# A second weight group's loads moved behind three activation loads, and its conversion behind the last unit's scaling, in a gated linear attention and feed-forward kernel

## The chip, the cores and the metric

One Trainium2 chip, one core. The metric is the device time of one launch in microseconds (us), lower is better. A reading is the median of several runs; the profile is one more execution, taken by the hardware profiler.

## The reference

Gated linear attention over 4 batches, 8 heads, 768 steps, 48 channels, then a feed-forward block with a leaky ReLU:

```python
for t in range(S):
    state = alpha[:, :, t, :, None] * state + np.einsum('bhd,bhe->bhde', k[:, :, t], v[:, :, t])
    y[:, :, t] = np.einsum('bhd,bhde->bhe', q[:, :, t], state)
...
x = np.ascontiguousarray(attn_out.transpose(0, 2, 1, 3)).reshape(B * S, H * D)   # 3072 x 384
h = x @ w_in                                                                    # w_in 384 x 2048
g = np.maximum(0.01 * h, h)
return (g @ w_out).astype(np.float32)                                           # w_out 2048 x 384
```

The weights arrive as 64-bit floats, all else as 32-bit ones.

## The kernel before

The steps are cut into 6 blocks of 128, and a **unit** is one block of one batch: 24 units, in the order block by block, batch by batch. Three units make one block of 384 rows for the feed-forward part, which takes the hidden width in 16 **weight groups** f of 128. One pair (block of rows i, weight group f) is an item: `ffn_in` (9 matmuls, L714), the leaky ReLU and the split of its result into a high and a low part (L719 to L728), `ffn_out` (9 matmuls, L743). A high part and two low ones give each product in three matmuls.

The attention of the first nine units, 0 to 8, runs ahead of nearly all feed-forward work; this stretch, some 65 us, is the one that the change touches. For one unit u:

- SyncE issues the loads: alpha, q and k (`load`, L151) and v (`load_values`, L170), 192 KB each. They go into ring buffers, so a load is issued when its buffer is free; "spare" is the third buffer of such a ring.
- TensorE transposes alpha, q and k (L303). VectorE scans alpha forward (`pc`, four short scans) and backward (`rc`, one long scan, in `scans`), and multiplies: `qs` = q times `pc` (`scaled_q`), `ks` = k times `rc` (`scaled_k`). A helper issues all of these, so they all stand as L288.
- TensorE makes the scores from `qs` and `ks` (L540); ScalarE copies them to `sm` (L420) and GpSimd zeroes their upper triangle (L422, both in `mask_scores`); TensorE transposes `ks` (`k_tokens`, L437), and ScalarE copies that and takes two sums (L441, L367).
- TensorE adds up the part of the past state (`past`), of the masked scores (`values`) and the new products (`products`), all L540; ScalarE and VectorE split the result into `large` (`split`, L554 and L288). After units 2, 5 and 8 two transfers inside the chip (`gather`, L603) bring the block of rows into place.

TensorE takes them in this order: scores(u), k_tokens(u), the transposes of u+1, past(u), values(u), products(u), scores(u+1).

Each weight group is loaded by five transfers on the same SyncE queue (`load_weights`): one of 384 KB of w_out (L228) and four of w_in (L224, 384 KB in all), into `raw`. Then it is **converted** from 64-bit to two 32-bit parts (`converting`, L241 to L280): ScalarE scales `raw` (L260) and takes the `signs` (L262); VectorE joins the `bits` (L266); ScalarE rounds them to the high part (L269); four VectorE operations (L273 to L280) give the low part.

A scheduler puts the instructions of every engine in an order, and the hardware keeps to it: each engine's queue is served in order. The kernel's text steers that order with `behind(key)`, which lets what stands in its block come behind a named earlier instruction of the same engine, and by the place at which the text gives an instruction out. Three tables do this for the first weight groups:

```python
LOADS = [(("v", 4), 0, 0), (("v", 5), 0, 1), (("v", 6), 1, None), (("g", 1), 2, None), (("v", 8), 3, None)]
AFTER = {0: ("sm", 5), 1: ("xh", 6), 2: ("sm", 8)}
BEGIN = ("sm", 5), ("xh", 6), ("kt", 8)
```

`LOADS` says behind which load a weight group's loads are issued: group 0 in two parts behind v of units 4 and 5, group 1 behind v of unit 6. `AFTER` puts the first ScalarE step of a conversion (L260) behind another ScalarE copy: for group 1 behind the split of unit 6. `BEGIN` says which instruction must have been given out before a conversion is.

Of the kernel before, what the change touches and what calls it, by code (L numbers as in the profile page):

```python
# [17 lines left out]
ALU = mybir.AluOpType  # L18
# [6 lines left out]
def gated_linear_attn_ffn(ctx, tc, q, k, v, alpha, w_in, w_out, out):  # L25
    nc = tc.nc
# [34 lines left out]
    AHEAD = 3 * UPB  # L61
# [54 lines left out]
    made = {}  # L116
# [3 lines left out]
    def behind(*key):  # L120

        return tc.issue_after(made[key].ins) if key in made else nullcontext()
# [7 lines left out]
    def load_next(u, i):  # L130

        for n in range(u + 1, u + 4):
            if n < NU and n - len(places(n, i)) == u:
                load(n, i)
# [28 lines left out]
    def load_values(u):  # L163
        if u >= NU:
            return
        if u >= AHEAD and later is not None:
            later.append((load_values, u))
            return
        tb, b = units[u]
        made["v", u] = nc.sync.dma_start(  # L170
            vals_sb[u % NV].rearrange("t (h d) -> t h d", h=H),
            v[b, :, tb * C:(tb + 1) * C, :].rearrange("h t d -> t h d"),
        )
# [58 lines left out]
    def put(ordered, eng, op, *args):  # L232

        if not ordered:
            return op(*args)
        line = lines[eng]
        with tc.issue_after(line[-1].ins) if line else nullcontext():
            line.append(op(*args))
        return line[-1]

    def converting(f, ordered=False):  # L241

        if f >= NF:
            return
        raw = jobs.pop(f)
        w_sb[f] = cst.tile([P, 2, 2 * DM], F32R, name=f"w{f}")
        hi, lo = w_sb[f][:, HIGH, :], w_sb[f][:, LOW, :]
        if not f64:
            val = raw[:, :, 0:P].bitcast(F32)
            hi, lo = (t.rearrange("p (g f) -> p g f", f=P) for t in (hi, lo))  # L250
            nc.scalar.copy(hi, val)
            made["w", f] = nc.vector.tensor_tensor(lo, val, hi.bitcast(F32), ALU.subtract)
            return
        words = raw.rearrange("p g (f w) -> p (g f) w", w=2)
        top, low = words[:, :, 1], words[:, :, 0]
        bits = cvp.tile([P, 2 * DM], I32, name="bits", bufs=NBITS)
        val = bits.bitcast(F32)

        with nullcontext() if lines["ACT"] else behind(*AFTER.get(f, ("hi", f - 1))):
            put(ordered, "ACT", lambda: nc.scalar.mul(top.bitcast(F32), top.bitcast(F32), 2.0 ** -112))  # L260
        yield
        put(ordered, "ACT", lambda: nc.scalar.copy(  # L262
            signs.bitcast(F16).rearrange("p (n w) -> p n w", w=2)[:, :, 1], top.bitcast(F32)))
        yield
        with nullcontext() if ordered else behind("w", f - 1):
            put(ordered, "DVE", lambda: nc.vector.scalar_tensor_tensor(  # L266
                bits, top, 3, signs, ALU.logical_shift_left, ALU.bitwise_or))
        yield
        made["hi", f] = put(ordered, "ACT", lambda: nc.scalar.copy(hi, val))  # L269
        yield  # L270
        pw = cvp.tile([P, 2 * DM], I32, name="pw", bufs=NPW)
        rest = pw.bitcast(F32)
        put(ordered, "DVE", lambda: nc.vector.tensor_scalar(pw, bits, -0x800000, None, ALU.bitwise_and))  # L273
        yield
        put(ordered, "DVE", lambda: nc.vector.tensor_tensor(val, val, hi.bitcast(F32), ALU.subtract))
        yield
        put(ordered, "DVE", lambda: nc.vector.scalar_tensor_tensor(
            rest, low.bitcast(U32), 2.0 ** -52, rest, ALU.mult, ALU.mult))
        yield
        made["w", f] = put(ordered, "DVE", lambda: nc.vector.tensor_tensor(lo, rest, val, ALU.add))  # L280

    def convert(f):
        for _ in converting(f):
            pass

    def vector(u, op, *args):

        return put(u >= AHEAD, "DVE", lambda: op(*args))  # L288
# [4 lines left out]
    def transposed(u, i, name, **kw):  # L293

        src = loaded(u, i)
        if u < AHEAD:
            ps = banks4()
            tiles = [ps[:, p, :] for p in range(NP)]
            if u == 0 and i == 0:
                other = ps_h.tile([P, 512], F32, name="ph").rearrange("r (p n) -> r p n", p=NP)  # L300
                tiles[NP // 2:] = [other[:, p, :] for p in range(NP // 2)]
            for p in range(NP):
                last = nc.tensor.transpose(  # L303
                    tiles[p], by_token(src)[:, 2 * p:2 * p + 2, :].rearrange("t h d -> t (h d)"), ident
                )
                if u == 0 and p % 2:
                    with tc.issue_after(last.ins):
                        keep_warm(WARM[2 * i + p // 2])
            return [ps, other] if u == 0 and i == 0 else ps
        t = atp.tile([P, NP, C], F32, name=name, **kw)  # L310
        src = src.rearrange("r (p n) -> r p n", p=NP)[:, :, 0:RUN]
        vector(
            u, nc.vector.transpose, t.rearrange("r p (j t) -> r p t j", t=T4),
            src.rearrange("r p (t d) -> r p t d", t=T4)[:, :, :, 0:32],
        )
        return t
# [11 lines left out]
    def every(t, first):  # L328
        return t.rearrange("r p (m s) -> r p m s", s=STEP)[:, :, :, first]

    def scans(u):
        aT = transposed(u, 0, "e", bufs=1)
        yield TURN
        pc, rc = (
            atp.tile([P, NP, C], F32, name=name, bufs=2 if u < AHEAD else 1) for name in (("pc", "rc") if u < AHEAD else ("up", "down"))
        )
        pe = ends_sb[u % 3]
        parts = aT if isinstance(aT, list) else [aT]
        n = NP // len(parts)
        for p in range(NP):  # L340
            vector(
                u, nc.vector.tensor_tensor_scan, pc[:, p, :], parts[p // n][:, p % n, :], ones.broadcast_to([P, C]), 1.0,
                ALU.mult, ALU.mult,
            )
        yield SCAN
        for part in parts:
            vector(u, nc.vector.memset, every(part[:, 0:n], 0), 0.0)
        vector(u, nc.vector.reciprocal, every(seed, STEP - 1), every(pc, STEP - 1))
        for at, part in zip(range(0, NP, n), parts):
            flat = [t.rearrange("r p t -> r (p t)") for t in (part[:, 0:n], seed[:, at:at + n], rc[:, at:at + n])]  # L350
            last = seed[:, at + n - 1, C - 1:C]
            nc.gpsimd.tensor_copy(rc[:, at + n - 1, C - 1:C], last)
            vector(
                u, nc.vector.tensor_tensor_scan,
                flat[2][:, n * C - 2::-1], flat[0][:, n * C - 1:0:-1], flat[1][:, n * C - 2::-1], last, ALU.mult, ALU.add
            )
        load_next(u, 0)
        nc.gpsimd.tensor_copy(pe, pc[:, :, C - 1:C])  # L358
        live[u] = [pc, rc, pe]
        sums[u] = pc, rc  # L360
        yield SCAN
# [7 lines left out]
    def scaled_q(u):  # L369
        pc = live[u][0]  # L370
        qT = transposed(u, 1, "qs")
        yield TURN
        load_next(u, 1)
        qs = qT if u >= AHEAD else atp.tile([P, NP, C], F32, name="qs")
        vector(u, nc.vector.tensor_tensor, qs, qT, pc, ALU.mult)
        live[u].append(qs)
        yield PASS

# [267 lines left out]
    def attention_later(first, last):  # L646

        def prepared(u):

            if u < last:  # L650
                yield from chain(scans(u), scaled_q(u), scaled_k(u))
                sum_up(u)
# [116 lines left out]

    LOADS = [(("v", 4), 0, 0), (("v", 5), 0, 1), (("v", 6), 1, None), (("g", 1), 2, None), (("v", 8), 3, None)]

    AFTER = {0: ("sm", 5), 1: ("xh", 6), 2: ("sm", 8)}

    BEGIN = ("sm", 5), ("xh", 6), ("kt", 8)

    STARTS = {62: ("kt", 7), 69: ("kt", 8)}
    st = attention(0, AHEAD)
# [1 line left out]
    for n, _ in enumerate(st):  # L781
        if n == 2:
            load_values(NV - 1)
        while LOADS and LOADS[0][0] in made:
            key, f, part = LOADS.pop(0)
            with behind(*key):
                load_weights(f, part)
            loaded_f = f + 1
        u = AHEAD - EARLY + converted
        if converted < EARLY and all(key in made for key in (("ks", u), BEGIN[converted])):  # L790
            with behind("ks", u):
                convert(converted)
            converted += 1
        if n in STARTS:
            i, f = items[len(gs)][:2]
# [20 lines left out]
    for n in range(len(items) + LAG):  # L816
        if n < len(items):
            i, f, _, _ = items[n]
# [36 lines left out]
        if n >= LAG:  # L855
            i, f, _, tag = items[n - LAG]
# [142 lines left out]
```

## Time and profile before

| what | value |
|---|---|
| median of 3 runs | 512.28 us (511.42 to 513.10) |
| profiled execution, its own time | 511.95 us |
| its span, first to last instruction | 510.2 us |
| TensorE busy (matmul) | 496.7 us, 97% of the span |
| VectorE / ScalarE / GpSimd busy | 372.0 / 250.8 / 67.9 us |
| mean granted TensorE clock | 0.997 of full speed |

The profiled execution's time is 1.75 us over its span, and 0.33 us under the median of the runs. Times in the rows below are microseconds from the first instruction. A busy TensorE says only that some matmul was in flight. In rows of a timeline the columns are the start, the busy time, the engine, the line, the operation, what it writes and reads, its shapes and a count of merged instructions; in brackets stands how long the engine was idle just before, and what ended that.

### The profile page before, as it was taken

The page shows a single profiled execution, that of the slowest core. Times are in us where ns is not written, and L with a number is a line of the kernel's source. Part 1 is how long each engine was busy: PE and PEld are TensorE (multiplying, and loading weights), DVE is VectorE, ACT ScalarE, POOL GpSimd, SP SyncE. Part 2 cuts the span into 40 slices and gives each one's busy share as a digit, 9 for nine tenths or more (in the row PEclk, how much of TensorE's full clock was granted, in tenths as well). Part 3 has the DMA queues.
Part 4 walks back from the last instruction along what each step waited for, and adds up shares of the span by engine and source line. Part 5 has one row for each costly group of instructions (what it writes and reads, how often), then busy time and mean ns, then how long its engine had stood idle before and what let it go on. Part 6 is the DMA issues. An engine that isn't in the chain of part 4 may idle for free.

```text
span 510.2 us, 12216 instructions
## 1 busy us (share of the span) xinstructions
PE 496.7 (97%) x4906; PEld 480.4 (94%) x4906; DVE 372.0 (73%) x700; ACT 250.8 (49%) x524; POOL 67.9 (13%) x161
## 2 busy tenths in 40 slices
PE   8997899999999999999999999999999999999996
PEld 7786799999999999999999999999999999999996
DVE  7999789999999768776768678676877674333331
ACT  2665777767664534444443543344443543334331
POOL 5454400000001111102201112101101100000000
PEclk9999899999999999999999999999999999999999
DMA  9999976777403423524324333243421101001001
GB/s 145 168 182 178 220 173 155 206 169 188 85 1 100 142 62 82 122 61 120 75 58 99 87 90 74 56 99 92 101 58 40 37 14 26 1 0 48 0 1 51
DMA packets 92990, 46.77 MB, mean 92 GB/s; under 512 B 57856, under 2 KB 90112, under 8 KB 92928
## 3 DMA queue, kind: packets, MB, share of 16 engines
q1 hardware_dynamic: 92928, 45.93, 41.1%
q8 instruction: 40, 0.66, 0.6%
q14 instruction: 22, 0.18, 0.1%
HBM read 38.83 MB, written 4.72 MB: 85 GB/s over the span
## 4 chain that ended last, share of the span: by engine, by line
PE 90%; DMA 4%; DVE 2%; SPq 1%; ACT 1%; issue 1%; POOL 0%; ACTq 0%; DVEq 0%
PE ph L714 39%; PE b L743 34%; PE a L540 6%; PE a L743 5%; PE ph L540 2%; PE a L437 2%; PE b L540 2%; DMA small<-in_alpha_dram 1%; PE b L303 1%; DMA raw<-in_moe_w_in_dram 1%; DMA large<-large 1%; DMA small<-in_k_dram 1%; PE a L303 1%; DVE rc L288 0%; DVE ks L288 0%
## 5 line engine op out<-in xcount | busy, mean ns | idle before, releaser
L714 PE MATMUL ph<-large,w 128*128 128x384 f32 x1152 | 225.8, 337 | 0.7 <-DMA large<-large 0.7
L714 PEld LDWEIGHTS ph<-large,w 128*128 128x128 f32 x1152 | 201.7, 189 | 1.8 <-ACT gh L724 1.0
L743 PE MATMUL b<-w,gh 128*128 128x384 f32 x672 | 168.2, 337 | 0.0
L722 DVE TENSOR_TENSOR t<-ph,t 128x384 f32<-128x384 f32 x128 | 70.5, 550 | 73.4 <-ACT t L719 73.3
L743 PEld LDWEIGHTS b<-w,gh 128*128 128x128 f32 x672 | 119.9, 188 | 1.1
L719 ACT ACTIVATE t<-ph 128x384 f32<-128x384 f32 x128 | 62.6, 489 | 116.0 <-PE ph L714 115.9
L724 ACT CAST gh<-t 128x384 fp32r<-128x384 f32 x128 | 65.7, 514 | 94.3 <-DVE t L722 94.1
L743 PE MATMUL b<-w,gl 128*128 128x384 f32 x336 | 108.2, 334 | 0.0
L728 DVE TENSOR_TENSOR gl<-t,gh 128x384 fp32r<-128x384 f32 x128 | 70.6, 551 | 31.2 <-ACT gh L724 31.2
L743 PEld LDWEIGHTS b<-w,gl 128*128 128x128 f32 x336 | 62.7, 188 | 0.0
L422 POOL TENSOR_SCALAR_AFFINE_SELECT sm<-sm 64x256 f32<-64x256 f32 (+1 forms) x48 | 25.6, 542 | 45.9 <-ACT sm L420 41.9
L288 DVE TENSOR_TENSOR_SCAN down<-e,small 128x511 f32<-128x511 f32 x15 | 19.3, 1285 | 5.3 <-DMA out_dram<-o 4.9
L535 POOL MEMSET small<- 128x1 f32 x15 | 1.5, 99 | 153.0 <-PE a L540 140.2
L540 PE MATMUL a<-qs,ks 48*64 48x64 f32 (+1 forms) x552 | 20.9, 228 | 0.2 <-ACT ktok L441 0.2
L743 PE MATMUL a<-w,gh 128*128 128x384 f32 x96 | 20.5, 334 | 0.0
L288 DVE TENSOR_TENSOR_SCAN up<-e,small 128x128 f32<-128x128 f32 x60 | 20.4, 402 | 0.1
L540 PEld LDWEIGHTS a<-qs,ks 48*64 48x64 f32 (+1 forms) x552 | 17.7, 141 | 1.6 <-issue 1.1
L358 POOL COPY small<-up 128x4 f32<-128x4 f32 x15 | 5.9, 394 | 95.8 <-DVE up L288 95.8
L262 ACT CAST signs<-raw 128x768 f16<-128x768 f32 x16 | 17.2, 1076 | 0.1
L743 PEld LDWEIGHTS a<-w,gh 128*128 128x128 f32 x96 | 17.0, 188 | 0.0
L288 DVE STREAM_TRANSPOSE e<-small 128x512 f32<-128x512 f32 x15 | 16.9, 1125 | 0.0
L266 DVE SCALAR_TENSOR_TENSOR bits<-raw,signs 128x768 int32<-128x768 int32 x16 | 15.2, 952 | 1.9 <-ACT signs L262 1.9
(113 smaller groups left out, 607.7 us busy)
## 6 DMA issues: line engine op xcount, KB each, us to landing
raw<-in_moe_w_out_dram SPq DMA_DIRECT2D x16, 384.0 KB, 4.0
small<-in_v_dram SPq DMA_DIRECT2D x24, 192.0 KB, 3.8
raw<-in_moe_w_in_dram SPq DMA_DIRECT2D x32, 144.0 KB, 4.0
out_dram<-o SPq DMA_DIRECT2D x24, 192.0 KB, 2.4
small<-in_alpha_dram SPq DMA_DIRECT2D x32, 96.0 KB, 2.4
small<-in_q_dram SPq DMA_DIRECT2D x30, 96.0 KB, 2.2
small<-in_k_dram SPq DMA_DIRECT2D x30, 96.0 KB, 2.2
small<-in_alpha_dram SPq DMA_DIRECT2D x30, 80.0 KB, 2.2
```

The costliest lines, as they stand in the source:

```text
L262: put(ordered, "ACT", lambda: nc.scalar.copy(signs.bitcast(F16).rearrange("p (n w) -> p n w", w=2)[:, :, 1], top.bitcast(F32)))
L266: put(ordered, "DVE", lambda: nc.vector.scalar_tensor_tensor(bits, top, 3, signs, ALU.logical_shift_left, ALU.bitwise_or))
L288: return put(u >= AHEAD, "DVE", lambda: op(*args))
L303: last = nc.tensor.transpose(tiles[p], by_token(src)[:, 2 * p:2 * p + 2, :].rearrange("t h d -> t (h d)"), ident)
L422: made["mask", u] = nc.gpsimd.affine_select(out=sm[s][part], in_=sm[s][part], compare_op=ALU.is_ge, fill=0.0, base=0, pattern=[[0, NP], [1 ...
L540: made["product",] = nc.tensor.matmul(out, weights, moving, start=start, stop=stop, skip_group_check=True)
L714: product = nc.tensor.matmul(ph, w_in_of(f, wn, g), xt[:, g, :], start=n == 0, stop=n == 3 * NG - 1)
L719: put(ordered, "ACT", lambda: nc.scalar.mul(t, ph, 0.01))
L722: put(ordered, "DVE", lambda: nc.vector.tensor_tensor(t, ph, t, ALU.max))
L724: put(ordered, "ACT", lambda: nc.scalar.copy(gh, t))
L728: made["gl", i, f] = put(ordered, "DVE", lambda: nc.vector.tensor_tensor(gl, t, gh.bitcast(F32), ALU.subtract))
L743: product = nc.tensor.matmul(po[j], gt[:, js], w_out_of(f, wn), start=f == 0 and n == 0, stop=f == NF - 1 and n == 2)
```

## The change

Three things. The loads of weight group 1 are issued behind v of unit 7, where they were behind v of unit 6. The first VectorE step of the conversions of groups 0 and 1 (L266) gets a place of its own: for group 0 behind the reversed scan of unit 7, for group 1 behind the multiplication `qs` of unit 8 (a new table, `SCANNED`, and two entries of `made` that name these instructions). And these two conversions are given out later (`BEGIN`). `AFTER`, the place of the first ScalarE step, stays.

```diff
-        with nullcontext() if ordered else behind("w", f - 1):
+        with nullcontext() if ordered else behind(*SCANNED.get(f, ("w", f - 1))):
             put(ordered, "DVE", lambda: nc.vector.scalar_tensor_tensor(
                 bits, top, 3, signs, ALU.logical_shift_left, ALU.bitwise_or))
...
-            vector(
+            made["rc", u] = vector(
                 u, nc.vector.tensor_tensor_scan,
...
-        vector(u, nc.vector.tensor_tensor, qs, qT, pc, ALU.mult)
+        made["qs", u] = vector(u, nc.vector.tensor_tensor, qs, qT, pc, ALU.mult)
...
-    LOADS = [(("v", 4), 0, 0), (("v", 5), 0, 1), (("v", 6), 1, None), (("g", 1), 2, None), (("v", 8), 3, None)]
+    LOADS = [(("v", 4), 0, 0), (("v", 5), 0, 1), (("v", 7), 1, None), (("g", 1), 2, None), (("v", 8), 3, None)]
     AFTER = {0: ("sm", 5), 1: ("xh", 6), 2: ("sm", 8)}
-    BEGIN = ("sm", 5), ("xh", 6), ("kt", 8)
+    SCANNED = {0: ("rc", AHEAD - 2), 1: ("qs", AHEAD - 1)}
+    BEGIN = ("rc", 7), ("qs", 8), ("kt", 8)
```

What this does to the order of the instructions, at three places.

SyncE's queue, from the load of v of unit 6 (the first row) to that of unit 8; "spare" is k and then q of unit 8:

```order
 L170 DMA small<-in_v_dram 128x8x48
-L228 DMA raw<-in_moe_w_out_dram 128x384
-L224 DMA raw<-in_moe_w_in_dram 48x3x128 x2
-L224 DMA raw<-in_moe_w_in_dram 16x3x128 x2
 L151 DMA spare<-in_k_dram 128x8x48
 L151 DMA spare<-in_q_dram 128x8x48
-L170 DMA small<-in_v_dram 128x8x48 x2
+L170 DMA small<-in_v_dram 128x8x48
+L228 DMA raw<-in_moe_w_out_dram 128x384
+L224 DMA raw<-in_moe_w_in_dram 48x3x128 x2
+L224 DMA raw<-in_moe_w_in_dram 16x3x128 x2
+L170 DMA small<-in_v_dram 128x8x48
```

The five loads of weight group 1 have gone behind three others: k and q of unit 8 and v of unit 7. Only v of unit 8 stands behind them still.

VectorE, unit 8's reversed scan and its two multiplications; before:

```order
L288 RECIPROCAL small<-pc 128x32
L266 SCALAR_TENSOR_TENSOR bits<-raw,signs 128x768
L288 SCALAR_TENSOR_TENSOR rc<-b,small 128x511
L273 TENSOR_SCALAR pw<-bits 128x768
L288 TENSOR_TENSOR ks<-a,rc 128x512
L277 SCALAR_TENSOR_TENSOR pw<-raw,pw 128x768
L288 TENSOR_TENSOR qs<-b,pc 128x512
```

and with the change:

```order
L288 RECIPROCAL small<-pc 128x32
L288 TENSOR_TENSOR large<-b,large 112x4x128
L288 SCALAR_TENSOR_TENSOR rc<-b,small 128x511
L288 TENSOR_TENSOR ks<-a,rc 128x512
L288 TENSOR_TENSOR qs<-b,pc 128x512
L266 SCALAR_TENSOR_TENSOR bits<-raw,signs 128x768
L722 TENSOR_TENSOR t<-ph,t 128x384
```

The conversion of weight group 1 no longer stands between unit 8's scan and its multiplications, but behind them all (the row `large`, the split of unit 6, stood just ahead of the reciprocal before).

ScalarE, from the split of unit 6 (first row) to the first leaky ReLU, with the change:

```order
L554 CAST large<-b 112x4x128
L260 ACTIVATE raw<-raw 128x768
L262 CAST signs<-raw 128x768
L420 COPY sm<-a 128x512
L420 COPY sm<-b 128x512
L441 COPY ktok<-a 128x448
L367 ACTIVATE pc,small<-pc 128x512
L367 ACTIVATE rc,small<-rc 128x512
L719 ACTIVATE t<-ph 128x384
```

Here only the last row is new, the rounding of group 1's high part (L269) stood ahead of it and is now behind it. The two rows of weight group 1 (L260, L262) stand ahead of the two copies of unit 7's scores (L420), as they did.

## Rows read from the trace of the kernel before

**Rows 1.** The page's part 4: shares of the span by engine, along the chain that ended last.

```profile
PE 90%; DMA 4%; DVE 2%; SPq 1%; ACT 1%; issue 1%; POOL 0%; ACTq 0%; DVEq 0%
```

**Rows 2.** TensorE's waits from 60 us to the end, the longest: who waited for whom, total, times, longest.

```profile
PE ph L714 <- DMA large<-large: 0.7, 1, 0.7
```

**Rows 3.** Stretches: start and end, length, then busy time (and instructions) of TensorE's matmuls, its weight loads, VectorE, ScalarE and GpSimd, then the granted TensorE clock, the DMA engines' busy share and GB/s.

```profile
56.50:58.70 2.20, 0.64 (x20) 0.51 (x16) 2.20 (x5) 1.37 (x3) 0.00 (x0) 1.00 1.01 250
60.20:63.70 3.50, 3.50 (x16) 3.06 (x16) 2.05 (x4) 3.50 (x9) 2.55 (x3) 0.51 1.03 267
66.70:94.00 27.30, 27.30 (x160) 27.29 (x158) 26.90 (x43) 20.68 (x32) 0.00 (x0) 1.00 0.69 166
```

**Rows 4.** The chain that ended last, in order of time, around 46 to 78 us: start, length, what.

```profile
46.01 5.56 DMA raw<-in_moe_w_in_dram
...
51.67 0.93 ACT raw L260
...
53.72 0.96 DVE bits L266
54.68 1.19 DVE rc L288
...
58.12 0.61 DVE qs L288
...
58.77 0.37 PE b L540
...
60.51 2.91 PE ph L714 x9
...
75.82 1.56 PE ph L714 x9
```

**Rows 5.** VectorE's timeline: the joining of the bits of weight groups 0 and 1, the low part of group 1, and the second leaky ReLU.

```profile
42.15 0.96 DVE L266 SCALAR_TENSOR_TENSOR bits<-raw,signs 128x768 int32<-128x768 int32 x1 [0.36 <-ACT signs L262]
...
53.72 0.96 DVE L266 SCALAR_TENSOR_TENSOR bits<-raw,signs 128x768 int32<-128x768 int32 x1 [1.11 <-ACT signs L262]
...
60.24 0.94 DVE L280 TENSOR_TENSOR w<-pw,bits 128x768 fp32r<-128x768 f32 x1
...
64.43 0.56 DVE L722 TENSOR_TENSOR t<-ph,t 128x384 f32<-128x384 f32 x1 [2.19 <-ACT t L719]
```

**Rows 6.** TensorE's timeline: values of unit 6 (first row); past of unit 7, its values (two rows) and products.

```profile
48.65 0.42 PE L540 MATMUL b<-sm,small 128*64 128x128 f32 x4 [1.27 <-DMA small<-in_v_dram]
...
54.19 1.09 PE L540 MATMUL b<-qs,small 112*64 112x128 f32 x16
55.23 0.43 PE L540 MATMUL b<-sm,small 128*64 128x128 f32 x4
55.81 0.87 PE L540 MATMUL b<-sm,small 128*64 128x128 f32 x12 [0.15 <-POOL sm L422]
56.51 0.62 PE L540 MATMUL a<-small,ktok 128*48 128x48 f32 x16
```

**Rows 7.** ScalarE's timeline: the first step of weight group 0, and the copies of unit 7's scores. And GpSimd's: the masking of these.

```profile
40.10 0.93 ACT L260 ACTIVATE raw<-raw 128x768 f32<-128x768 f32 x1 [0.79 <-DMA raw<-in_moe_w_in_dram]
...
53.56 0.58 ACT L420 COPY sm<-a 128x512 f32<-128x512 f32 x1
54.02 0.60 ACT L420 COPY sm<-b 128x512 f32<-128x512 f32 x1
...
54.21 1.55 POOL L422 TENSOR_SCALAR_AFFINE_SELECT sm<-sm 128x512 f32<-128x512 f32 x2 [1.36 <-ACT sm L420]
```

**Rows 8.** SyncE's timeline, DMA issues: the start and how long the issue took. The loads are q of unit 1; v of unit 1; v of unit 4 and w_out of weight group 0; v of unit 5; v of unit 6; v of units 7 and 8 in one row.

```profile
4.02 0.88 SPq L151 DMA_DIRECT2D small<-in_q_dram  x1
...
10.89 1.05 SPq L170 DMA_DIRECT2D small<-in_v_dram  x1
...
27.09 0.81 SPq L170 DMA_DIRECT2D small<-in_v_dram  x1
27.95 1.30 SPq L228 DMA_DIRECT2D raw<-in_moe_w_out_dram  x1
...
32.41 0.87 SPq L170 DMA_DIRECT2D small<-in_v_dram  x1
...
41.29 0.54 SPq L170 DMA_DIRECT2D small<-in_v_dram  x1
...
48.59 3.27 SPq L170 DMA_DIRECT2D small<-in_v_dram  x2
```

**Rows 9.** DMA issues, each taken alone: the transfer, count, size, and us from the start of the issue to the landing. In the order of rows 8: q of unit 1, v of unit 1, v of unit 4, w_out of group 0, v of units 5, 6 and 7.

```profile
small<-in_q_dram SPq DMA_DIRECT2D x1, 192.0 KB, 4.9
...
small<-in_v_dram SPq DMA_DIRECT2D x1, 192.0 KB, 5.0
...
small<-in_v_dram SPq DMA_DIRECT2D x1, 192.0 KB, 4.3
...
raw<-in_moe_w_out_dram SPq DMA_DIRECT2D x1, 384.0 KB, 4.6
...
small<-in_v_dram SPq DMA_DIRECT2D x1, 192.0 KB, 6.7
...
small<-in_v_dram SPq DMA_DIRECT2D x1, 192.0 KB, 7.2
...
small<-in_v_dram SPq DMA_DIRECT2D x1, 192.0 KB, 5.2
```

## The prediction

> **What bounds the kernel now.** I read the page's chain first: 90% of it is TensorE [rows 1]. The question is only from which moment on. TensorE's waits after 60 us answer it: the longest is 0.7 us, a transfer inside the chip [rows 2], and from 66.7 to 94 us matmuls cover all 27.30 us [rows 3]. So from unit 8's scores on, which start at 58.77 us [rows 4], the rest is a solid block of matmul work: whatever moves that start moves the end by as much, if no new wait comes behind it.
>
> Next, the chain just before 58.77 us [rows 4]. Weight group 1's last load lands at 46.01 + 5.56 = 51.57 us; ScalarE scales `raw`, takes the signs, VectorE joins the bits at 53.72 after an idle 1.11 us [rows 5], and only behind that come unit 8's reversed scan and `qs`, which release the scores. This is the wait that the change aims at. But TensorE also has to finish values and products of unit 7 before it may take these scores, and they end at 56.51 + 0.62 = 57.13 us [rows 6]. So the VectorE wait is only 58.77 - 57.13 = **1.64 us later** than the next limit, and no gain from this move alone can be larger.
>
> What sets that next limit? Values of unit 7 need masked scores: GpSimd's masking starts at 54.21, as soon as ScalarE's copy at 53.56 is done, and TensorE waits 0.15 us for it between its two rows [rows 6, 7]. That copy stands on ScalarE right behind the two steps of weight group 1, which wait for the load. So unit 7's values, too, hang on the landing of the weights: they end 57.13 - 51.57 = **5.56 us after it**. On ScalarE the change leaves this order as it was. And it sends the loads later.
>
> **The change, part by part.** It adds and removes no operation.
>
> *Bits of groups 0 and 1, moved on VectorE.* For group 0 an idle 0.36 us before the bits goes away ahead of unit 7's scan [rows 5]. I cost this at nothing: behind it TensorE waits 1.27 us for v of unit 6, until 48.65 [rows 6], which the change doesn't issue earlier. If that load came 1.3 us sooner, the 0.36 us would count. For group 1 the 1.11 us of waiting and the conversion's steps leave unit 8's path. Its `qs` then follows its `rc` and `ks` directly, and can be done by about 55.3 us: `rc` of 1.19 us behind the reciprocal, the transposes just ahead of past of unit 7 at 54.19, then two multiplications of some 0.6 us [rows 4, 6]. VectorE is out of the chain there, with some 4 us to spare.
>
> *Group 1's five loads, moved behind three loads.* They pass k and q of unit 8 and v of unit 7, which now start earlier. When do the weights land? v of unit 6, just ahead in both orders, lands at 41.29 + 7.2 = 48.5 us [rows 8, 9]. From there I bound the rest from both sides.
>
> - Upper end, by loads in a full queue: from q to v of unit 1, six loads apart, landings go from 4.02 + 4.9 = 8.9 to 10.89 + 5.0 = 15.9 us, 1.16 us each [rows 8, 9]. Three make 3.5. w_out of group 0 lands 1.2 us behind v of unit 4 (32.6 against 31.4), and its w_in some 0.9 us behind v of unit 5 (39.1; ScalarE starts at 40.10) [rows 7 to 9]. Together 48.5 + 3.5 + 1.2 + 0.9 = 54.1. Group 1 itself took longer, 51.57 - 48.5 = 3.1 us instead of 2.1, which gives 55.1; with some stall 55.5.
> - Lower end, by the end of the stretch itself: v of unit 7, last of the three, landed at 48.59 + 5.2 = 53.8, only 2.2 us behind the weights, as the three were partly served beside them [rows 8, 9]. 48.5 + 2.2 + 2.1 = 52.8.
> - The same eight transfers, in the other order and with a queue that is never empty, should be done when they were done before: 53.8.
>
> I take **54.0**, nearest to the last, since it is this stretch's own; the ends 52.8 and 55.5 stay for the range.
>
> The Trainium skill has a price for that, too ("DMA: Bandwidth & Descriptors", section Specifications): a fabric ceiling of 435 GB/s, and full rate only from 512 bytes per descriptor up. By the ceiling alone the three loads are an estimated 1.4 us, the weights would land near 52.9, and the kernel would come out at 512.0. The row of 1.16 us for 192 KB is 170 GB/s, in 192-byte pieces, so the trace sides with the page's second clause.
>
> *What follows.* Weights at 54.0 put the end of unit 7's values and products at 54.0 + 5.56 = 59.56, and unit 8's scores at about 59.6 us, released by TensorE itself. Against 58.77 that is **+0.8 us**. The 1.64 us are gained and 2.4 us of later landing lost.
>
> *What is late next.* Group 1's bits start 53.72 - 51.57 = 2.15 us behind the landing, so at 56.2 us, and the low part was done 60.24 + 0.94 - 53.72 = 7.5 us behind the bits [rows 4, 5]: 63.7 us, if the steps between are spaced as they were. Its first use stands behind unit 8's values in the new order, shortly ahead of the solid block that began at 66.7 [rows 3]: covered by some 2 us. VectorE's idle 2.19 us before the second leaky ReLU [rows 5] takes up the delay. The transfers of `gather` and unit 8's v are issued earlier; nobody waits for them.
>
> *The clock.* From 60.2 to 63.7 us the granted clock was 0.51, that is the lower level of 1.2 GHz, behind a stretch in which TensorE was busy for 0.64 of 2.20 us [rows 3]. Nine matmuls took 2.91 us there and 1.56 later [rows 4], so this costs 1.4 us. With the change the idle time lies between past of unit 7, at 55.3, and its values, at 54.0 + 3.66 = 57.7: 2.4 us instead of 1.6. I expect the clock to fall once again, at the same price: no change in the sum.
>
> **The sum.** The profiled execution took 511.95 us; 511.95 + 0.8 = 512.8. It lies 0.33 us under the median of the runs, so against that I forecast 512.28 + 0.8 = **513.1 us**: slightly slower, but within the 0.3% (1.5 us) that a measurement of this kernel can tell from no change.
>
> **The rivals.**
>
> *The loads moved ahead cost almost nothing.* Weights by 52.8 to 53.2. For it: the three landed within 2.2 us. Against it: the 1.16 us a load wherever the queue was full. Then scores come at 52.8 + 5.6 = 58.4, 0.4 us early: 511.9. If besides the clock doesn't fall, 510.5.
>
> *The clock doesn't fall, weights as I forecast.* For it: TensorE also sat idle 1.27 us before unit 6's values [rows 6], without a fall. Against it: the idle stretch grows. 513.1 - 1.4 = 511.7.
>
> *Slower: ScalarE's queue.* The load lands late, ScalarE stands at L260, and unit 7's score copies, masks and values with it. For it: group 1 took 3.1 us in this very stretch. It decides from a landing at 54.7 us on (54.7 + 5.6 - 58.8 = 1.5 us). At 55.5 the scores start at 61.1, +2.3: 514.6.
>
> *Slower by the clock.* It falls for twice as long, since the idle stretch and the thin work behind it are longer: 513.1 + 1.4 = 514.5.
>
> That the change doesn't do what it says is out: the order of VectorE's instructions shows it done.
>
> **How the numbers follow.** Weights between 53.2 and 54.7, clock as before: 0.47. Cheap loads: 0.20. No fall of the clock: 0.10. ScalarE's queue: 0.18. The longer fall: 0.05. Faster than 510.7 needs cheap loads and the full clock together, or more than I see: 0.13 in all. Slower than 513.8 are the last two, and the upper edge of the first: 0.25. The rest, 0.62, is no change. The range goes from the cheap loads with full clock, 510.7, to the late landing at 514.6 with some of the runs' spread, 514.9.
>
> **What would show it.** Right: in the profile after, the chain ahead of unit 8's scores goes through the w_in load, L260, L262, L420 and the masks, no longer through L266; the wait of TensorE before unit 7's values is over 2 us, ended by GpSimd or ScalarE; `qs` of unit 8 is done some 4 us before its scores. Wrong: group 1's last load lands before 53 us, or ScalarE's L260 is not what unit 7's copies stand behind, or TensorE's block of work begins at another place than unit 8's scores, or the clock falls not once, as before, but never or for longer.

## The result, and the profile after

| | kernel before | changed kernel |
|---|---|---|
| median of 10 runs | 512.69 us | **515.03 us** (513.91 to 518.06) |
| ratio of the times, 95% interval | | 1.0067 [1.0040, 1.0094] |
| profiled execution, own time / span | 511.95 / 510.2 us | 513.91 / 512.5 us |
| mean granted clock of the runs | 0.995 to 1.000 in 73 of 76 later runs | 0.997 down to 0.988 |

One execution of the kernel before read 2759.88 us; the ratio leaves it out, the median in the table does not (the other nine have 512.37). By the ratio the change makes the kernel slower by 0.7%, some 3.4 us, where 513.1 and "no change that can be told" were forecast; the medians, 515.03 against 512.37, are 2.7 us apart. A second measurement later gave 1.0087 [1.0062, 1.0113], some 4.5 us.

The page of the changed kernel, its span and its chain:

```profile
span 512.5 us, 12195 instructions
...
PE 85%; DVE 8%; issue 2%; DMA 1%; ACT 1%; POOL 1%; SPq 1%; DVEq 0%; ACTq 0%; POOLq 0%
```

Against [rows 1] TensorE's share of the chain fell and VectorE has 8% of it. TensorE's longest waits between 60 and 180 us, as [rows 2]:

```profile
PE a L540 <- ACT ktok L441: 0.5, 1, 0.5
PE ph L714 <- DVE w L280: 0.2, 1, 0.2
```

0.7 us in all; the second of them is explained below. The next view is the timeline from the landing of group 1's weights to the first feed-forward work. The rows are in groups by engine: ScalarE, GpSimd, TensorE (values in two rows and products of unit 7, scores of unit 8, then the item (1, 0)), VectorE.

```profile
53.88 0.90 ACT L260 ACTIVATE raw<-raw 128x768 f32<-128x768 f32 x1 [4.18 <-DMA raw<-in_moe_w_in_dram]
54.81 1.04 ACT L262 CAST signs<-raw 128x768 f16<-128x768 f32 x1
55.72 0.57 ACT L420 COPY sm<-a 128x512 f32<-128x512 f32 x1
...
56.37 1.56 POOL L422 TENSOR_SCALAR_AFFINE_SELECT sm<-sm 128x512 f32<-128x512 f32 x2 [4.79 <-ACT sm L420]
...
57.39 0.43 PE L540 MATMUL b<-sm,small 128*64 128x128 f32 x4 [3.17 <-POOL sm L422]
57.98 1.20 PE L540 MATMUL b<-sm,small 128*64 128x128 f32 x12 [0.15 <-POOL sm L422]
58.95 1.05 PE L540 MATMUL a<-small,ktok 128*48 128x48 f32 x16
59.93 0.58 PE L540 MATMUL b<-qs,ks 48*128 48x128 f32 x1
...
62.27 1.81 PE L714 MATMUL ph<-large,w 128*128 128x384 f32 x9
...
53.80 0.68 DVE L288 TENSOR_TENSOR qs<-b,pc 128x512 f32<-128x512 f32 x1
55.88 0.96 DVE L266 SCALAR_TENSOR_TENSOR bits<-raw,signs 128x768 int32<-128x768 int32 x1 [1.40 <-ACT signs L262]
...
65.98 0.56 DVE L722 TENSOR_TENSOR t<-ph,t 128x384 f32<-128x384 f32 x1 [1.90 <-ACT t L719]
```

Up to here it went as forecast. The last load landed at 53.78 us (forecast: 54.0). ScalarE stood idle for it for 4.18 us, with unit 7's score copies behind; GpSimd and TensorE's values follow in a chain, and TensorE idles 3.17 us before them. VectorE is out of it: `qs` of unit 8 is done at 54.5 us, 5.4 us before the scores. These start at 59.93 us, where 58.77 stood in [rows 4]: +1.16 us, with 59.6 forecast.

Two things are new. The first is where the clock falls. The windows' columns are the stretch, its length, the busy time (and count) of TensorE's matmuls and weight loads, VectorE, ScalarE and GpSimd, then the granted clock, the DMA engines' busy share and GB/s:

```profile
54.10:57.35 3.25, 0.12 (x4) 0.00 (x0) 1.34 (x2) 3.22 (x6) 0.98 (x2) 1.00 1.00 227
...
58.38:61.79 3.41, 3.41 (x42) 3.24 (x37) 2.76 (x5) 2.06 (x5) 0.02 (x1) 0.50 0.99 218
...
125.00:140.00 15.00, 14.91 (x86) 14.60 (x85) 13.82 (x23) 9.55 (x15) 1.18 (x1) 1.00 0.49 102
140.00:155.00 15.00, 14.76 (x84) 14.16 (x83) 14.91 (x24) 8.78 (x17) 0.00 (x0) 1.00 0.00 1
```

Half the clock is granted from 58.38 us on, behind a stretch in which TensorE was busy 0.12 of 3.25 us, and it falls on values, products and scores. In the kernel before it came at 60.3 and fell on the item (1, 0) [rows 3, 4]. That item now takes 1.81 us in place of 2.91, which gives most of the +1.16 back: at 72 us TensorE is only 0.52 us behind the kernel before, counted from matmul to matmul, and still 0.56 at 137 us.

The second new thing comes then. At 152.6 us TensorE is 1.53 us behind; the windows show it no longer covered, 14.91 and 14.76 of 15.00 us, where the kernel before has

```profile
125.00:140.00 15.00, 15.00 (x89) 15.00 (x88) 14.63 (x25) 9.49 (x17) 1.14 (x1) 1.00 0.47 92
140.00:155.00 15.00, 15.00 (x87) 14.79 (x86) 14.42 (x23) 9.15 (x16) 0.00 (x0) 1.00 0.01 2
```

The place is VectorE's reversed scan of unit 9, the first unit behind the nine. VectorE's and TensorE's rows around it:

```profile
135.77 0.32 DVE L288 RECIPROCAL small<-up 128x32 f32<-128x32 f32 x1
135.79 0.09 DVE L288 MEMSET e<- 128x32 f32 x1
137.08 1.28 DVE L288 TENSOR_TENSOR_SCAN down<-e,small 128x511 f32<-128x511 f32 x1 [1.00 <-PE b L743]
...
135.84 1.20 PE L743 MATMUL b<-w,gh 128*128 128x384 f32 x6
136.88 1.37 PE L714 MATMUL ph<-large,w 128*128 128x384 f32 x7
```

and the same scan in the kernel before, on VectorE:

```profile
135.21 0.31 DVE L288 RECIPROCAL small<-up 128x32 f32<-128x32 f32 x1
135.23 0.09 DVE L288 MEMSET e<- 128x32 f32 x1
135.56 1.28 DVE L288 TENSOR_TENSOR_SCAN down<-e,small 128x511 f32<-128x511 f32 x1
```

The scan (`down<-e`) starts 0.35 us behind the reciprocal in the kernel before. In the changed kernel it stands 1.00 us idle, until TensorE's six matmuls of L743 end at 137.04 us. The two built programs say why; in their lists of VectorE's instructions with their waits, the scan has one more:

```
before:   L288 SCALAR_TENSOR_TENSOR down<-e,small 128x511 [waits DVE_49]
changed:  L288 SCALAR_TENSOR_TENSOR down<-e,small 128x511 [waits DVE_49,PE_49]

tile (128 rows)           byte address in each row, before    changed
down of unit 9            217216                              217216
gh of item (0, 11)        209024                              217216
```

The scan computes with nothing of TensorE's. But its output tile takes over the place in SBUF of the `gh` that those matmuls read, so it has to wait until they are done. In the kernel before, that `gh` lay elsewhere. The change moves no instruction here. The ones that it moves stand some 70 us earlier; with them the allocator handed out the places of later tiles in another order. It is the move of the conversions that does it: with the loads alone moved (e3 below) this `gh` stays at 209024 and the scan does not wait, with the conversions alone (e2) it lies at 217216 and the scan waits.

How VectorE's 1.00 us comes to TensorE, in the rows of its weight loads:

```profile
138.87 1.54 PEld L714 LDWEIGHTS ph<-large,w 128*128 128x128 f32 x9 [0.41 <-DVE t L722]
...
153.16 0.30 PEld L714 LDWEIGHTS ph<-large,w 128*128 128x128 f32 x2 [0.28 <-DVE t L722]
154.03 1.17 PEld L714 LDWEIGHTS ph<-large,w 128*128 128x128 f32 x7 [0.57 <-DVE w L280]
```

VectorE has no gap in which to catch up: it is busy for 14.91 of the 15.00 us from 140 us on. The next leaky ReLU (`t`) is late at 138.9 us, and at 153.2 and 154.0 us the leaky ReLU and a weight group's low part (L280, the wait of 0.2 us above). Those are the steps in which TensorE's lateness grows from 0.56 to 1.53 us. The profile's span is 2.3 us longer than that of the kernel before; 1.2 us of this stand at the last matmul. The rest is the end behind it, 4.2 us before and 5.3 us here, which varies from 4.15 to 6.10 us over all profiled executions, whatever the version.

### The profile page after: what moved, and what is told of

It is laid out like the page before. It is cut to its first block, busy times and chain, and to the rows that moved or that the text cites. A ratio compares the mean times of both kernels' runs of the same rounds, so it can differ in the third digit from the quotient of the medians.

```text
span 512.5 us, 12195 instructions
## 1 busy us (share of the span) xinstructions
PE 497.9 (97%) x4906; PEld 480.8 (94%) x4906; DVE 371.1 (72%) x700; ACT 250.0 (49%) x524; POOL 67.2 (13%) x161
## 4 chain that ended last, share of the span: by engine, by line
PE 85%; DVE 8%; issue 2%; DMA 1%; ACT 1%; POOL 1%; SPq 1%; DVEq 0%; ACTq 0%; POOLq 0%
PE ph L714 34%; PE b L743 32%; PE a L540 6%; PE a L743 3%; PE b L540 2%; PE b L303 2%; PE ph L540 2%; PE a L437 1%; DVE gl L728 1%; DVE ks L288 1%; DVE qs L288 1%; PE a L303 1%; DVE pc L288 1%; DMA raw<-in_moe_w_in_dram 1%; DVE t L722 1%
## 5 line engine op out<-in xcount | busy, mean ns | idle before, releaser
L743 PE MATMUL b<-w,gh 128*128 128x384 f32 x672 | 168.4, 337 | 0.0
L743 PEld LDWEIGHTS b<-w,gh 128*128 128x128 f32 x672 | 120.0, 188 | 1.1
L743 PE MATMUL b<-w,gl 128*128 128x384 f32 x336 | 108.1, 334 | 0.0
L743 PEld LDWEIGHTS b<-w,gl 128*128 128x128 f32 x336 | 62.7, 188 | 0.0
L540 PE MATMUL a<-qs,ks 48*64 48x64 f32 (+1 forms) x552 | 22.0, 230 | 0.3 <-ACT ktok L441 0.2
L743 PE MATMUL a<-w,gh 128*128 128x384 f32 x96 | 20.5, 334 | 0.0
L262 ACT CAST signs<-raw 128x768 f16<-128x768 f32 x16 | 17.1, 1072 | 0.1
L743 PEld LDWEIGHTS a<-w,gh 128*128 128x128 f32 x96 | 17.0, 188 | 0.0
L260 ACT ACTIVATE raw<-raw 128x768 f32<-128x768 f32 x16 | 14.6, 915 | 4.2 <-DMA raw<-in_moe_w_in_dram 4.2
```

The costliest lines, as they stand in the source:

```text
L262: put(ordered, "ACT", lambda: nc.scalar.copy(signs.bitcast(F16).rearrange("p (n w) -> p n w", w=2)[:, :, 1], top.bitcast(F32)))
L540: made["product",] = nc.tensor.matmul(out, weights, moving, start=start, stop=stop, skip_group_check=True)
L743: product = nc.tensor.matmul(po[j], gt[:, js], w_out_of(f, wn), start=f == 0 and n == 0, stop=f == NF - 1 and n == 2)
```

## The experiments

Ten runs in three groups (e1 to e4, e5 to e8, e9 and e10), each group beside the kernel before on the same chip (medians 511.59, 511.92 and 511.79 us). "Late" is how far matmuls of the feed-forward part start behind those of the kernel before's profile; the scan's wait is VectorE's idle time before unit 9's reversed scan.

| run | median us | ratio [95%] | unit 8's scores at | late at 137 / 152.6 us | scan's wait |
|---|---|---|---|---|---|
| changed kernel | 515.03 | 1.0067 [1.0040, 1.0094] | 59.93 | +0.56 / +1.53 | 1.00 |
| the same again (e6) | 516.49 | 1.0087 [1.0062, 1.0113] | 60.95 | +3.47 / +4.44 | 1.00 |
| loads alone (e3) | 514.43 | 1.0061 [1.0036, 1.0086] | 62.47 | +2.71 / +2.71 | 0 |
| conversions alone (e2) | 511.53 | 0.9999 [0.9980, 1.0018] | 57.44 | -1.02 / -0.06 | 1.00 |
| changed, L260 behind unit 7's copies (e1) | 510.89 | 0.9996 [0.9974, 1.0018] | 55.59 | -2.64 / -2.48 | 0 |
| changed, fill on TensorE (e4) | 519.42 | 1.0162 [1.0131, 1.0193] | 60.25 | +4.05 / +4.16 | 0 |
| changed, `gh` first (e5) | 514.61 | 1.0052 [1.0030, 1.0073] | 61.40 | +1.59 / +1.60 | 0 |
| conversions alone, `gh` first (e7) | 509.59 | 0.9965 [0.9951, 0.9978] | 55.59 | -3.11 / -3.11 | 0 |
| the same again (e10) | **509.15** | **0.9955** [0.9933, 0.9976] | 55.88 | -3.08 / -3.08 | 0 |
| e1 with the loads as before (e8) | 510.64 | 0.9975 [0.9955, 0.9995] | 57.09 | -0.84 / -0.66 | 0 |
| before, `gh` first (e9) | 512.22 | 1.0013 [0.9991, 1.0035] | 58.62 | -1.13 / -1.03 | 0 |

"Late" compares single executions, and two things that vary from one to the next stand in it. The kernel before's profile has a fall of the clock at 60.3 us, while e9, with the same order of instructions and the same idle 1.64 us ahead of the scores, has none, and leads by 1.1 us at 137 us with no change in its runs. The profiles of e1, e2, e7, e8 and e10 have none either, so about 1 us of each of their leads may be this. The other is the landing of v of unit 6, for which TensorE waits: 47.4 to 49.2 us over the executions. What happens between two moments of one execution is the firmer reading.

**Loads alone (e3).** The kernel before with

```diff
-    LOADS = [..., (("v", 6), 1, None), ...
+    LOADS = [..., (("v", 7), 1, None), ...
```

> Before with the loads of group 1 moved behind v of unit 7 and nothing else. Theory A: the load lands at 53.8; bits at 56.0 still stand ahead of unit 8's reversed scan on VectorE, so unit 8's scores start near 61, 2.2 us later than before: 514.5 to 515.5. Rival B: the loads cost nothing without the late conversion, 512.5.

514.43 us, 1.0061: the move of the loads by itself costs what the whole change costs. Unit 8's scores start at 62.47 us, released by `qs` again, since the conversion still stands ahead of it. The granted clock falls twice:

```profile
48.78:52.19 3.41, 2.88 (x34) 2.82 (x36) 2.51 (x7) 0.46 (x1) 0.77 (x1) 0.50 0.99 229
...
59.02:62.43 3.41, 2.87 (x32) 2.35 (x32) 3.41 (x6) 2.66 (x7) 0.92 (x2) 0.50 1.00 249
```

**Conversions alone (e2).** The changed kernel with the loads behind v of unit 6 again:

> The change with its loads undone: group 1 is loaded behind v of unit 6 as before, only the conversions are moved. Theory A: the load lands at 51.6, unit 7's values and products end at 57.1, unit 8's scores start there instead of at 58.8, so 1.6 us under before, near 511. Rival B: the late conversion costs by itself, and the time is that of the change, 514 to 515. Rival C (VectorE's wait was hidden anyway): as before, 512.5.

511.53 us, no change, where a gain of 1.6 was expected. (The profiled execution, 512.81 us, is the slowest of its runs.) The scores start 1.3 us earlier, near the 57.1 us expected, but of TensorE's lead of 1.02 us at 137 us 0.06 is left at 152.6. This was the first sign that something behind the stretch takes time back; the changed kernel's scan stands there as well:

```profile
134.19 0.32 DVE L288 RECIPROCAL small<-up 128x32 f32<-128x32 f32 x1
...
135.50 1.28 DVE L288 TENSOR_TENSOR_SCAN down<-e,small 128x511 f32<-128x511 f32 x1 [1.00 <-PE b L743]
```

**ScalarE's queue (e1).** The changed kernel with group 1's L260 and L262 behind unit 7's score copies:

```diff
-    AFTER = {0: ("sm", 5), 1: ("xh", 6), 2: ("sm", 8)}
+    AFTER = {0: ("sm", 5), 1: ("sm", 7), 2: ("sm", 8)}
```

> The change, with one entry of AFTER turned as well: the first ScalarE step of weight group 1 (L260) comes behind unit 7's score copies and token copy, where it stood ahead of them. Theory A (ScalarE's queue: unit 7's copies stand behind two steps that wait for the load): the copies start at about 50.3 us instead of 55.7, values of unit 7 follow its past at 54.2 without a wait, unit 8's scores start at about 56 us (59.9 with the change, 58.8 before), and the kernel comes out 2 to 3 us under before, near 510. Rival B (the late conversion on VectorE is what costs, wherever ScalarE's copies stand): bits of group 1 stay at 56 us or later, TensorE waits for the low part of group 1, and the time stays near that of the change, 514 to 515.

510.89 us: by the ratios, 0.9996 against 1.0067, some 3.6 us for one entry of a table, though it is no faster than the kernel before beyond its interval. ScalarE's and TensorE's rows:

```profile
50.39 0.59 ACT L420 COPY sm<-a 128x512 f32<-128x512 f32 x1 [0.54 <-PE b L540]
...
54.09 0.93 ACT L260 ACTIVATE raw<-raw 128x768 f32<-128x768 f32 x1 [0.97 <-DMA raw<-in_moe_w_in_dram]
...
55.59 0.37 PE L540 MATMUL b<-qs,ks 48*128 48x128 f32 x1
```

The copies no longer stand behind the load, unit 7's values follow at once, the scores start at 55.59 us with the weights landing as late as in the changed kernel (53.99 us), and the clock does not fall in the middle of this execution. That unit 7's values hang on the landing only through ScalarE's queue is shown. Its scan carries a wait for TensorE as well, but on an earlier `gh`, long read.

**Fill for the clock (e4).** The changed kernel with unit 7's past computed four times over, the same result each time:

```diff
-                multiply([past(u), values(u), products(u)])
+                multiply([list(past(u))] * (4 if u == 7 else 1) + [values(u), products(u)])
```

> The change, with unit 7's past computed four times over on TensorE (the same products into the same place, the last counts), some 3 us of matmul work in the gap of 3.2 us before unit 7's values. Theory K (part of the loss is the clock, which falls over unit 8's scores because of that gap): the granted clock stays at the upper level, the scores take 1.1 us and not 2.0, the second leaky ReLU on VectorE comes about 1 us earlier, and the time is 1 to 2 us under the change's, near 513.5; the runs also lie closer together. Rival: the clock has no part in it, and the time is that of the change or a little over it (514.5 to 515.5).

519.42 us. The clock did stay full through values, products and scores, up to 66.04 us. But the scheduler put unit 7's state update (L575) and the split behind it (`large`) after the last conversion step of group 1 (presumably it counts the fill as work, which was not tested), and TensorE's next past waits for them (VectorE's rows, then TensorE's):

```profile
63.66 1.38 DVE L280 TENSOR_TENSOR w<-pw,bits 128x768 fp32r<-128x768 f32 x1
64.96 0.34 DVE L575 TENSOR_TENSOR small<-us,a 112x192 f32<-112x192 f32 x1
65.22 0.68 DVE L288 TENSOR_TENSOR large<-b,large 112x512 fp32r<-112x512 f32 x1
...
66.05 1.95 PE L540 MATMUL a<-qs,small 112*64 112x128 f32 x16 [2.51 <-DVE large L288]
```

The clock then fell behind that idle time. By 480 us TensorE is 6.8 us late; 4.2 of them are there by 152.6 us, what adds the rest stays open. The run tells nothing of the price of the clock; it tells that a fill is not neutral to an order that a scheduler makes.

**The place in memory (e5).** The changed kernel with two lines of `ffn_in` swapped, so that `gh` is reserved ahead of `t`. The instructions stand in the same order on all five engines. Addresses differ, and with them what some 80 instructions of VectorE, ScalarE and GpSimd wait for, unit 9's scan among them; none of these stands ahead of 85 us.

```diff
+        gh = ffp.tile([P, TB], F32R, name="gh", bufs=LAG + 1)
         t = ffp.tile([P, TB], F32, name="t")
...
-        gh = ffp.tile([P, TB], F32R, name="gh", bufs=LAG + 1)
```

> The changed kernel, with the tile gh of ffn_in reserved ahead of t; the order of the instructions is the same on every engine, only the places in SBUF differ. In the changed kernel unit 9's reversed scan (L288, down<-e) stood 1.00 us idle at 136 us for matmuls of L743, and its tile down has the address of the gh that these matmuls read; the kernel before has another tile there. Theory (the place in memory): the wait of 1.00 us is gone here, TensorE's lateness against the kernel before, +0.5 at 137 us, stays +0.5 to +0.8 at 174 us instead of growing to +2.0, and the time is 1.0 to 1.5 us under the changed kernel's (513.5 to 514.2 if that gives 515.0). Rival (VectorE has no slack, and hands its 1.55 us of lateness on by itself): TensorE is still 1.5 to 2.0 us late at 174 us, and the time is within 0.5 us of the changed kernel's.

VectorE's scan, and the two windows that had lost their cover:

```profile
136.80 0.32 DVE L288 RECIPROCAL small<-up 128x32 f32<-128x32 f32 x1
...
137.16 1.28 DVE L288 TENSOR_TENSOR_SCAN down<-e,small 128x511 f32<-128x511 f32 x1
```

```profile
125.00:140.00 15.00, 15.00 (x89) 15.00 (x87) 14.78 (x24) 10.14 (x17) 1.14 (x1) 1.00 0.58 115
140.00:155.00 15.00, 15.00 (x87) 14.78 (x87) 14.98 (x24) 8.89 (x16) 0.00 (x0) 1.00 0.00 1
```

The wait is gone, TensorE is covered throughout, and its lateness stays as it was: +1.59 us at 137, +1.60 at 152.6. The rival, that VectorE without slack hands its delay on, is out. In the runs the swap brought 1.9 us (514.61 against 516.49 on the same chip); among runs with a mean clock of 0.995 or more it is 1.4 us (medians 513.35 of 5 and 514.71 of 9), among those with 0.991 or less 1.5 us (515.98 of 5 and 517.47 of 6), and 5 of 12 runs are in the second group as 6 of 16 were, so nothing says that the swap works by the falls of the clock. The trace's own step is 0.97 us, the same to 0.02 us in all three executions with the wait. That the rest of the 1.4 us also belongs to this wait, and not to one of the other waits that the swap turns, is not shown.

**The changed kernel again (e6).**

> The changed kernel once more, for its clock and beside the other runs on the same chip. Its runs so far had mean clocks from 0.997 (513.91 and 515.14 us) to 0.988 (517.51 us), and the one profiled execution had one stretch of 3.41 us at half clock, in unit 8's scores. Theory (the clock): medians of 514.5 to 515.5 us, mean clocks spread from 0.988 to 0.997 again, the slower runs with the lower clocks; if the profiled execution is one of 0.995 or less it shows a second stretch at half clock, most likely at 48 to 53 us, where TensorE waits for unit 6's or 7's v and where the run with the loads alone had one. Rival (the clock plays no part; the placing of transfers does): times don't follow the clock, and a profile of 0.995 or less shows the lost clock elsewhere.

516.49 us. Its profiled execution took 516.97 us at a mean clock of 0.989, and shows where the clock went, though not where it was expected:

```profile
54.00:56.91 2.91, 0.80 (x16) 0.56 (x11) 1.10 (x3) 2.31 (x4) 0.00 (x0) 1.00 1.03 185
56.91:67.15 10.24, 9.09 (x65) 8.04 (x67) 5.66 (x9) 8.05 (x20) 4.92 (x6) 0.50 1.00 242
67.15:72.00 4.85, 4.85 (x61) 4.37 (x58) 3.76 (x7) 3.82 (x7) 0.00 (x0) 1.00 0.42 83
```

It is one fall, at the same idle time, but 10.24 us long and not 3.41, through scores, the items (1, 0) and (0, 1) and past of unit 8, with TensorE busy for 9.09 us of it. With the landing at 54.47 us, earlier than in e5 (54.90 us, a fall of 3.41 us), TensorE is 1.9 us later than there at 137 us. From 60.32 to 63.73 us a matmul was in flight throughout, and the clock stayed at half for another 3.42 us; in the changed kernel's first profile it rose behind such a stretch. Of the 16 runs of the changed kernel 6 have a mean clock of 0.991 or less, with a median of 517.47 us; the 9 with 0.995 or more have 514.71. Of 76 runs of the kernel before, one was so low. (The mean also counts a fall at the very end, behind the last matmul: e5's profile has 0.993 with the same 3.41 us, as its clock falls again at 509.4 us, while its last matmul ends at 507.1. For 0.991 that alone is too little.)

**Conversions alone, without the wait (e7, e10), and the control (e9).** e2 and the kernel before, each with the swap of e5.

> The conversions begun early with the loads as before (the second experiment), and gh reserved ahead of t. There the scan of unit 9 stood 1.00 us as well, and TensorE's lead on the kernel before went from 1.0 us at 132 us to 0.1 us at 152 us. Theory (the place in memory): no wait at the scan, a lead of 0.8 to 1.2 us still at 174 us, and 510.3 to 511.0 us where the kernel before gives 511.6 and the second experiment 511.5. Rival (VectorE without slack): the lead is gone by 174 us all the same, and the time is 511.3 to 511.9 us.

> The kernel before with gh reserved ahead of t and nothing else; the order of instructions is the same on every engine. In the kernel before unit 9's reversed scan does not wait for TensorE, and here its tile down follows a gh that matmuls of L743 have read some 2 us earlier. Theory (the edit helps only where the scan waits): no wait at the scan, and the kernel before's time within 0.3%, 511.3 to 512.5 us. Rival (the other places in memory are quicker for other reasons, and the gain of the run before was theirs): 509.5 to 510.5 us.

> The conversions begun early, the loads as before, gh ahead of t, once more and on the same chip as the run of the kernel before with gh ahead of t alone. Theory: 509.2 to 510.2 us again, ratio 0.994 to 0.998, mean clocks of 0.997 to 1.0, and 1.5 to 2.5 us under the kernel before with gh ahead of t. Rival (the first result was luck of the chip): 510.8 us or more.

509.59 and 509.15 us, ratios 0.9965 and 0.9955, both intervals below 1: this version beats both kernels. They are quicker than the 510.3 us that was the best expected of e7. Nor is it the clock alone: among runs with a mean clock of 0.998 or more the medians are 509.61 and 508.97 us, and 510.92 for the kernel before. The swap alone does nothing (e9, 1.0013). TensorE's and VectorE's rows in e10:

```profile
47.64 0.43 PE L540 MATMUL b<-sm,small 128*64 128x128 f32 x4 [0.76 <-DMA small<-in_v_dram]
...
55.88 0.37 PE L540 MATMUL b<-qs,ks 48*128 48x128 f32 x1
...
132.13 0.32 DVE L288 RECIPROCAL small<-up 128x32 f32<-128x32 f32 x1
...
132.48 1.28 DVE L288 TENSOR_TENSOR_SCAN down<-e,small 128x511 f32<-128x511 f32 x1
```

Scores at 55.9 us, no idle VectorE before the scan, and no fall of the clock before 505 us; all 24 runs have 0.997 or more. But these two profiles lead e2's by 2.1 us already at 137 us, ahead of the scan, and that is not the swap: v of unit 6 landed at 47.4 and 47.5 us here and at 49.2 in e2, whose row is

```profile
49.29 0.43 PE L540 MATMUL b<-sm,small 128*64 128x128 f32 x4 [1.27 <-DMA small<-in_v_dram]
```

In all five runs that have neither VectorE's wait nor the one on ScalarE's queue (e1, e2, e7, e8, e10) unit 8's scores start 7.9 to 8.2 us behind unit 6's values, which wait for this load. With both out of the way it is v of unit 6 that sets the scores.

**e1 with the loads as before (e8).**

> The conversions begun early, the loads as before (behind unit 6's v) and group 1's top words multiplied behind unit 7's score copies on ScalarE: the first experiment without the move of the loads. Theory (ScalarE's queue alone set the start of unit 8's scores): these start at 55.3 to 55.9 us as in the first experiment, since nothing before them waits for the load; the group being there earlier gives nothing more, and the time is that of the first experiment, 510.4 to 511.2 us. Rival (the load's landing still holds the first experiment back at its second leaky ReLU, 62.2 us): 0.5 to 1.5 us less, 509.5 to 510.3 us.

510.64 us, within the first expectation's time. But its scores came at 57.09 us and not 55.6, since v of unit 6 arrived 1.5 us later in that execution than in e1's: "nothing before them waits for the load" held for group 1's load, not for this one. Whether the earlier landing is worth anything here stays open: the intervals of e1 and e8 overlap.

## Why the prediction was wrong

The direction was right, the size was not: +0.8 us forecast, some +3.4 measured.

- *VectorE's wait was only 1.64 us above the next limit, and ScalarE's queue is that limit.* Right for the changed kernel: e1 moves only two steps on that queue and starts the scores 4.3 us earlier. With the loads as before it was one of two: unit 7's values followed its past within 0.15 us, and with the conversions moved (e2, e7, e10) they wait for nothing; TensorE's own work from v of unit 6 on is the limit there.
- *Landing at 54.0 us, with 52.8 to 55.5 as bounds.* Right in its bounds: 53.78, 54.47 and 54.90 us in the three executions with this order of all instructions, 53.99, 54.73 and 55.29 in e1, e4 and e3, which share the order of the loads. 54.0 was at the early side.
- *Values and products end 5.56 us behind the landing.* Mis-sized. The scores start 6.15, 6.48 and 6.50 us behind it, because the clock already falls during values and products. The estimate took durations at full clock from an execution in which the fall came later.
- *"I expect the clock to fall once again, at the same price: no change in the sum."* This step failed. The fall begins 1.9 us earlier, and 6 of 16 runs have a mean clock of 0.991 or less, where the profile shown first has 0.997 with one fall of 3.41 us; the one execution of these six that was profiled had 10.24 us. The rival "twice as long" had 0.05. (The price of one fall, put at 1.4 us, was nearer 1.0 between two executions of the same order: e9, without a fall, leads the kernel before by 1.13 us at 137 us, 0.15 of it at the scores.) Between the two groups of runs lie 2.8 us; 6/16 of that is 1 us on the mean.
- *"A solid block of matmul work: whatever moves that start moves the end by as much, if no new wait comes behind it."* This step failed too, by its own condition. A new wait came, at 136 us, where nothing was moved: 0.97 us in the trace, while taking it out by the swap brought about 1.4 us in the runs. The range allowed for other starts, not for this.
- *VectorE's idle 2.19 us takes up group 1's delay.* Right: TensorE nowhere waits for this group's low part, and e5 keeps its lateness through the stretch.

Together, as estimates from medians of runs: some 1.6 us by later scores, where 0.8 was forecast (e5 against the kernel before, runs at a clock of 0.995 or more, 513.35 against 511.75 us), 1.4 by the inherited places, 1 by the longer falls; the sum, 4.0, lies between the two measurements (3.4 and 4.5). What decides whether a fall lasts 3.41 or 10.24 us stays open.

The change itself was two changes of opposite sign. The conversions alone are worth -1.8 to -2.3 us with the swap (e7, e10), and nothing without it (e2); the loads alone cost +3.1 us (e3).

## What to carry to other kernels

Before an instruction order is changed, compare the waits of the two built programs over the whole kernel, not just the order near the edit: a tile may inherit another place far behind, and a wait for an engine that it has no data from is the sign to look at (e1's scan carries one too, at no cost). A load that is moved later should be followed to every queue in which an instruction waits for it; here the way out was to move the waiting instruction behind the copies, or not to move the load. And where an edit lengthens an idle stretch of TensorE, price the clock by its spread over several executions, not by one profile.

## What the runs showed of the hardware

After an idle stretch of about 3 us TensorE's granted clock fell to half for 3.41 us in two profiled executions of this order (changed kernel, e5) and for 10.24 us in a third, in which TensorE was busy for 9.09 us of them. I had taken the length of a fall for fixed. And the same order of instructions with the same idle 1.64 us was followed by a fall in one execution (the kernel before) and by none in another (e9).
